# A mixed SSM and MLP kernel: u stored in quarters, Bu's fourth product and the output block's second product put earlier

## Chip, cores and metric

The kernel runs on one core of a Trainium2 chip. The metric is device time in microseconds, from the first to the last instruction and what lies around them; lower is better. Engines are named as in the profile: PE does matmuls, PEld loads their weights, DVE is the vector engine, ACT the scalar engine, POOL is GpSimd, and SP issues loads.

## The reference

The input x has 2048 rows of 1024. One path is a diagonal complex state-space model: an input product Bu, a recurrence along the 2048 rows, and an output product with C. The other is a layer norm and an MLP of width 3584 with gelu. A gate for each row mixes them.

```python
Bu = jnp.einsum("bld,pd->blp", x + 0j, B_bar)
...
for t in range(L):
    h = Lam_bar[None, :] * h + Bu[:, t, :]
...
y = 2.0 * jnp.einsum("blp,dp->bld", hseq, Cmat).real + x * Dskip[None, None, :]
...
y = _layernorm(x, axis=-1)
h = _gelu(jnp.einsum("bsd,df->bsf", y, w1) + b1)
return jnp.einsum("bsf,fd->bsd", h, w2) + b2
...
return g * a + (1 - g) * b
```

## The kernel before

Every large product is cut in a two by two grid and done with seven products instead of eight, in the way of Strassen and Winograd. A group (class SG) has the seven as p1 to p7, in three PSUM banks: p1 and p2 share bank a, p5 and p3 share bank e, and p6, p7 and p4 share bank b. ACT copies p1's bank into bank b ahead of p6 (the seed, L904). ACT also copies bank e after p5 (s5) and bank b after p6 (su) to SBUF (L888, or L889 with a factor). The function fin of each kind of group takes the four results out: after p2, p3, p7 and p4. A later product on a bank waits until the earlier result in it has been read. Sums of inputs that S and T operands need are made by DVE (dve_tt, L932).

Four kinds of groups follow each other on PE. Bu groups (bu_group, 4 matmuls a product) make u for 8 tiles of 128 states, in two halves of the rows, after four plain products (bu_plain). Then come blocks of m groups (MLP up, 4 matmuls a product, gelu on ACT at L1318 and L1324, DVE's addition at L1322), b groups (MLP down, 7 matmuls, results at L1402 and L1405, stored to scr_ac as partial sums at L1412 and, accumulating, L1414), and at the end the 8 y groups (output product, 8 matmuls, results at L1501 and L1503). Products of neighbouring groups are interleaved: a group's p7 and p4 stand among the next group's products.

u goes from ACT and DVE (L1010, L1016, L1019 with L1021) to a ring of two slots in SBUF, and from there to scratch in HBM by stores on POOL's queue (u_store, L947). The scan (ssm, on DVE: L1198, L1201, L1212) loads u for four tiles and 256 rows at a time (L1185) and stores its result on POOL's queue (L1230). POOL also makes the layer norm's statistics (L1051 to L1056) and stores the normalised rows (L1063), which DVE makes at L1061.

The order on each engine isn't written by hand but for PE's. Each operation is a task with an engine, a guessed duration and a priority; PE's products are chained in the order in which the code makes them. Graph.schedule plays the tasks through with the guessed durations and fixes the order of every engine's list, SP's and POOL's queues among them. On the chip each engine works through its list in order and waits on semaphores. POOL_ISSUE is the guessed duration of a DMA issue on POOL. So a change of a guess or of PE's order can change the lists of all engines.

Buffers lie in one arena and overlap: the fourth of the sums for y groups with an even number (ysq, index 3) ends 1 KB inside the first slot of the ring from which the b groups' partial sums are stored. The planner makes the later writer wait for the earlier reader.

Of the kernel before, what the change touches and what calls it, by code (L numbers as in the profile page):

```python
# [25 lines left out]
ACT_ISSUE = 0.12  # L26
POOL_ISSUE = 1.2
XPOSE_ISSUE_PER_MB = 3.8
# [391 lines left out]
def build(nc, A_x, A_Lambda_re, A_Lambda_im, A_B_re, A_B_im, A_C_re, A_C_im, A_log_dt, A_Dskip,  # L420
          B_x, B_w1, B_b1, B_w2, B_b2, gate_w, out, stats=None):
# [5 lines left out]
    CH = 512  # L427
    NCH = L // CH
    DT = D // 128
    PT = P // 128  # L430
# [4 lines left out]
    T = 256  # L435
# [8 lines left out]
    g = Graph()  # L444
    es = ExitStack()
    with es:
# [9 lines left out]
        US = nc.dram_tensor("scr_u", (PT // 4, 128, L // T, 8 * T), BF16, kind="Internal").ap()  # L456
# [36 lines left out]
        EV0 = AO + 10240  # L493
# [440 lines left out]

        b_us = [[[B("us%d_%d_%d" % (p, c, r)) for r in range(2)] for c in range(NCH // 2)] for p in range(PT)]
        b_hs = [[B("hs%d_%d" % (p, h)) for h in range(L // T)] for p in range(PT // 4)]
# [6 lines left out]

        def u_store(pt, pr, ks, q, ri):
            evv = AR.v(EV0 + ks * 4096 + ri * 2048, [(T, 4), (1, T)])
            r0 = ((pt % 4) * 2 + ri) * T
            g.dma((1.0, q), lambda e: e.dma_start(out=US[pt // 4, :, 4 * pr:4 * pr + 4, r0:r0 + T], in_=evv.ap), 2 * 128 * CH * 2,  # L947
                  ssem("us", 2 * ks + ri, True), reads=[evv], writes=[b_us[pt][pr][ri]], name="us%d.%d.%d" % (pt, pr, ri), q="pool")

        cev = {}  # L950

        def bu_plain(pt, c):

            if c % 2 == 0:
                cev[pt, c // 2] = nxt("ev", NEV)
            ks = cev[pt, c // 2]
            for ri in range(2):
                bk = (4, 5, 6, 0, 1, 2)[nxt("cbank", 6)]
                ws = [AR.v(bqo(pt, 2 * ri) + dt * 256, [(1, 128)]) for dt in range(DT)]
                q = mm("bu%d.%d.%d" % (pt, c, ri), bk, ws, [xt(dt, c) for dt in range(DT)], True)  # L960
                ev = u_ev(pt, c // 2, ks, ri, c % 2)
                g.add("act", c_act(CH), (1.0, q), lambda e, ev=ev, bk=bk: e.activation(ev.ap, V(PS[bk], 0, [(1, 2 * T)]), AF.Copy),  # L962
                      reads=[b_ps[bk]], writes=[ev, b_ps[bk]], name="u%d.%d.%d" % (pt, c, ri))
                if c % 2 == 1:
                    u_store(pt, c // 2, ks, q, ri)

# [19 lines left out]
        def bu_group(pt, pr):  # L986
# [15 lines left out]
            bu_n[0] += 1  # L1002
            done = {}

            def fin(qd, q, bk):
# [6 lines left out]
                else:  # L1012
# [5 lines left out]
                    else:  # L1018
# [3 lines left out]
                              reads=[uc, sv], writes=[ev], name="u" + nm)  # L1022
                done[qd] = True
                if done.get(2 * ri) and done.get(2 * ri + 1):
                    u_store(pt, pr, ks, q, ri)
            return SG("_u%d.%d" % (pt, pr), st, mv, fin, su, s5)
# [99 lines left out]
        for n, (pt, pr) in enumerate(order):  # L1126
# [14 lines left out]
            cur.p5()  # L1141
            cur.p6()
            cur.p2()
            cur.p3()
            if prev is not None:
                prev.p4()
                opt = order[n - 1][0]
                if order[n - 1][1] == 1 and opt < 3:
                    bT_dma(opt + 5)
# [26 lines left out]
        def ssm(pg, q):  # L1176
# [5 lines left out]
            def pri(i):  # L1182
                return (50.0, un, i)
            uf = AR.v(so, [(1, UE)])
            g.dma((50.0, un), lambda e: e.dma_start(out=uf.ap, in_=US[pg, :, q, :]), UE * 128 * 2,  # L1185
                  ssem("sb", s), reads=[b_us[4 * pg + a][q // 4] for a in range(4)], writes=[uf], name="ul" + tag)

# [369 lines left out]
        for n, it in enumerate(flat):  # L1557
# [19 lines left out]
            if kind == "y":  # L1577
                if x + 1 < 8:
                    y_prep(x + 1, seq[0] + 4)
            early2 = kind == "b" and x == 0  # L1580
            if early2:
# [28 lines left out]
            if last_of_block:  # L1610
                if nit is None:
                    prev.p4()
                else:
                    nk = blocks[nit[0]][0]
                    if nk == "b":
# [9 lines left out]
                        pend = make((nit[0], nit[1] + 1))  # L1625
                        pend.p1()
                    else:
                        cur = make(nit)
# [59 lines left out]
```

## Time and profile before

| | |
|---|---|
| median of 3 runs | 558.57 us (558.56 to 558.93) |
| the profiled execution's own time | 558.57 us |
| its span | 556.8 us |
| PE busy | 548.0 us (98%) |
| DVE busy | 511.8 us (92%) |
| ACT busy | 283.1 us (51%) |
| POOL busy | 92.1 us (17%) |
| granted TensorE clock | 1.000 |

The span is the time from the first to the last instruction that the profile has; the execution's own time is 1.8 us longer. Busy time is summed over an engine's instructions. A row of a timeline gives start, duration, engine, line, operation and count; in brackets stands the idle time of the engine before it and what ended it. Consecutive instructions of DVE and ACT overlap by some 0.08 to 0.13 us. Matmuls overlap too, so a row's duration reaches a little into the next.

### The profile page before, as it was taken

The page shows a single profiled execution, that of the slowest core. Times are in us where ns is not written, and L with a number is a line of the kernel's source. Part 1 is how long each engine was busy: PE and PEld are TensorE (multiplying, and loading weights), DVE is VectorE, ACT ScalarE, POOL GpSimd, SP SyncE. Part 2 cuts the span into 40 slices and gives each one's busy share as a digit, 9 for nine tenths or more (in the row PEclk, how much of TensorE's full clock was granted, in tenths as well). Part 3 has the DMA queues.
Part 4 walks back from the last instruction along what each step waited for, and adds up shares of the span by engine and source line. Part 5 has one row for each costly group of instructions (what it writes and reads, how often), then busy time and mean ns, then how long its engine had stood idle before and what let it go on. Part 6 is the DMA issues. An engine that isn't in the chain of part 4 may idle for free.

```text
span 556.8 us, 7435 instructions
## 1 busy us (share of the span) xinstructions
PE 548.0 (98%) x2610; PEld 248.5 (45%) x2610; DVE 511.8 (92%) x867; ACT 283.1 (51%) x477; POOL 92.1 (17%) x146
## 2 busy tenths in 40 slices
PE   8999999989999999999999999999999999999997
PEld 5544444434444444444444444444444444444443
DVE  4999999999999999999999999999999867988873
ACT  3968899647774347674246753246662322111110
POOL 0226636630001110011110000220000211001000
DMA  9998999799492345576546866787669999686521
GB/s 263 243 310 204 260 283 275 235 354 328 151 226 97 135 185 181 169 233 230 208 163 197 284 142 156 140 196 196 201 159 257 233 286 320 215 325 238 191 99 57
DMA packets 114911, 120.08 MB, mean 216 GB/s; under 512 B 70322, under 2 KB 92594, under 8 KB 113850
## 3 DMA queue, kind: packets, MB, share of 16 engines
q1 hardware_dynamic: 102256, 73.69, 48.0%
q0 software_dynamic: 12480, 45.90, 26.5%
q8 instruction: 20, 0.33, 0.2%
q14 instruction: 17, 0.14, 0.1%
q10 hardware_dynamic: 138, 0.02, 0.0%
HBM read 56.40 MB, written 47.46 MB: 187 GB/s over the span
## 4 chain that ended last, share of the span: by engine, by line
PE 80%; DVE 13%; issue 2%; DMA 2%; POOL 2%; ACT 0%; DVEq 0%; ACTq 0%; POOLq 0%
PE ps L871 59%; PE ps L869 19%; DVE ar L932 3%; DMA scr_ac<-ar 2%; DVE ar L1212 2%; DVE ar L1198 2%; DVE ar L1061 1%; DVE ar L1016 1%; DVE ar L1021 1%; PE ps L686 1%; DVE ar L1201 1%; POOL cst L1052 1%; DVE ar L1322 1%; POOL scr_u L947 1%; DVE ar L852 1%
## 5 line engine op out<-in xcount | busy, mean ns | idle before, releaser
L871 PE MATMUL ps<-ar 128*128 128x512 f16 (+1 forms) x1832 | 414.3, 379 | 4.3 <-ACT ps L904 2.4
L871 PEld LDWEIGHTS ps<-ar 128*128 128x128 f16 (+1 forms) x1832 | 178.2, 98 | 223.2 <-ACT ps L904 4.2
L869 PE MATMUL ps<-ar 128*128 128x512 bf16 (+1 forms) x640 | 156.9, 379 | 0.1
L932 DVE TENSOR_TENSOR ar<-ar 128x512 f16<-128x512 bf16 (+6 forms) x216 | 138.9, 684 | 6.4 <-DMA scr_ac<-ar 4.9
L869 PEld LDWEIGHTS ps<-ar 128*128 128x128 bf16 (+1 forms) x640 | 62.2, 98 | 74.9 <-issue 0.4
L1212 DVE TENSOR_TENSOR_SCAN ar<-cst,init,ar 128x256 bf16<-128x256 f32 x128 | 88.8, 735 | 0.5
L888 ACT ACTIVATE ar<-ps 128x512 f32<-128x512 f32 x100 | 58.6, 594 | 50.2 <-PE ps L869 36.8
L1198 DVE TENSOR_TENSOR ar<-ar 128x2048 bf16<-128x2048 bf16 x64 | 77.0, 1218 | 0.1
L904 ACT ACTIVATE ps<-ps 128x512 f32<-128x512 f32 x66 | 38.5, 584 | 66.5 <-PE ps L869 61.9
L1318 ACT ACTIVATE ar<-ps,cst 128x512 bf16<-128x512 f32 x56 | 38.4, 687 | 21.5 <-PE ps L871 20.9
L889 ACT ACTIVATE ar<-ps,cst 128x512 f32<-128x512 f32 x32 | 22.0, 688 | 45.0 <-PE ps L871 19.3
L1324 ACT ACTIVATE ar<-ar,cst 128x512 bf16<-128x512 f32 x56 | 40.0, 714 | 7.7 <-DVE ar L1322 7.5
L1201 DVE TENSOR_TENSOR ar<-ar 128x1024 bf16<-128x1024 bf16 x64 | 42.7, 685 | 0.3
L1402 ACT ACTIVATE ar<-ps,cst 128x512 f32<-128x512 f32 x32 | 22.0, 687 | 41.2 <-PE ps L871 41.2
L1322 DVE TENSOR_TENSOR ar<-ps,ar 128x512 f32<-128x512 f32 x56 | 38.2, 682 | 3.3 <-PE ps L871 3.0
L947 POOL DMA_DIRECT2D scr_u<-ar x32 | 24.7, 774 | 62.1 <-ACT ar L962 22.8
L1503 DVE SCALAR_TENSOR_TENSOR ar<-ps,cst,ar 128x512 bf16<-128x512 f32 x32 | 23.8, 748 | 11.7 <-PE ps L871 11.6
L1230 POOL DMA_DIRECT2D scr_h<-ar x16 | 9.0, 564 | 125.4 <-DVE ar L1201 125.2
L1414 POOL DMA_DIRECT2D scr_ac<-ar x16 | 13.8, 892 | 81.2 <-DVE ar L1405 37.9
L1405 DVE SCALAR_TENSOR_TENSOR ar<-ps,cst,ar 128x512 f32<-128x512 f32 x32 | 23.8, 742 | 3.5 <-PE ps L871 3.2
L1482 DVE SCALAR_TENSOR_TENSOR ar<-ar,cst 128x1024 f32<-128x1024 bf16 x16 | 20.3, 1279 | 0.0
L1412 POOL DMA_DIRECT2D scr_ac<-ar x16 | 8.5, 532 | 69.2 <-DVE ar L1405 28.0
(110 smaller groups left out, 241.9 us busy)
## 6 DMA issues: line engine op xcount, KB each, us to landing
scr_ac<-ar POOLq DMA_DIRECT2D x32, 512.0 KB, 5.2
ar<-in_A_x_dram SPq DMA_DIRECT2D x32, 256.0 KB, 5.6
scr_u<-ar POOLq DMA_DIRECT2D x32, 256.0 KB, 5.3
ar<-scr_u SPq DMA_DIRECT2D x16, 512.0 KB, 5.2
scr_h<-ar POOLq DMA_DIRECT2D x16, 512.0 KB, 5.8
ar<-scr_ac SPq DMA_DIRECT2D x16, 512.0 KB, 6.9
ar<-scr_h SPq DMA_DIRECT2D x8, 1024.0 KB, 6.7
ar<-in_B_w_dram SPq DMA_DIRECT2D x14, 512.0 KB, 6.5
```

The source lines that it names most:

```text
L869: ins = e.matmul(V(PS[bk], 0, [(1, n)]), st[i].ap, mv[i].ap, start=(i == 0), stop=(i == K - 1))
L871: ins = e.matmul(V(PS[bk], 0, [(1, n)]), st[i].ap, mv[i].ap, start=False, stop=(i == K - 1), skip_group_check=True)
L888: return e.activation(o.ap, V(PS[bk], 0, [(1, 512)]), AF.Copy)
L904: g.add("act", c_act(512), (pb[0], q - 2), lambda e: e.activation(V(PS[b], 0, [(1, 512)]), V(PS[a], 0, [(1, 512)]), AF.Copy), reads=[b_ps[ ...
L932: g.add("dve", c_tt16(n), (pb[0], q), lambda e: e.tensor_tensor(o.ap, a.ap, b.ap, op), reads=[a, b], writes=[o], name=nm).slack = slack
L947: g.dma((1.0, q), lambda e: e.dma_start(out=US[pt // 4, :, 4 * pr:4 * pr + 4, r0:r0 + T], in_=evv.ap), 2 * 128 * CH * 2, ssem("us", 2 * ks ...
L1198: g.add("dve", c_tt16(UE), pri(i), lambda e: e.tensor_tensor(o.ap, a.ap, tbl.ap, ALU.mult), reads=[a, tbl], writes=[o], name=nm + tag)
L1201: g.add("dve", c_tt16(UE // 2), pri(i), lambda e: e.tensor_tensor(o.ap, a.ap, b.ap, op), reads=[a, b], writes=[o], name=nm + tag)
L1212: lambda e, pt=pt, ri=ri, vin=vin, go=go: e.tensor_tensor_scan(go.ap, Cb("R", pt, T), vin.ap, V(INIT, pt * 2 + ri, [(1, 1)]), ALU.mult, AL ...
L1318: g.add("act", c_act(512, ap_operands=1), (10.0, q + 1), lambda e: e.activation(o.ap, V(PS[bk], 0, [(1, 512)]), AF.Gelu_apprx_tanh, bias=C ...
L1322: g.add("dve", c_dve(512), (10.0, q - 2), lambda e: e.tensor_tensor(sv.ap, V(PS[bk], 0, [(1, 512)]), sv.ap, ALU.add), reads=[b_ps[bk], sv] ...
L1324: g.add("act", c_act(512, psum=False, ap_operands=1), (10.0, q + 3), lambda e: e.activation(o.ap, sv.ap, AF.Gelu_apprx_tanh, bias=C("B1", ...
```

## The change

Five edits. A store of u now carries 512 rows of one part (real or imaginary) of a tile and not 1024, and is issued as soon as these are there; 32 stores of 256 KB become 64 of 128 KB, with a semaphore each for the eight places of the ring, and a scan load waits only for the stores that hold its rows. POOL_ISSUE goes from 1.2 to 0.8. In the Bu loop the fourth product of the group before stands ahead of the second and third of the current one, and not behind them. At the start of the y block the first y group's second product stands ahead of its fifth, and the last b group's fourth stands ahead of both, where the fifth stood.

```diff
-POOL_ISSUE = 1.2
+POOL_ISSUE = 0.8
...
-        def u_store(pt, pr, ks, q, ri):
-            evv = AR.v(EV0 + ks * 4096 + ri * 2048, [(T, 4), (1, T)])
+        def u_store(pt, c, ks, q, ri):
+            evv = AR.v(EV0 + ks * 4096 + (ri * 4 + 2 * (c % 2)) * T * 2, [(T, 2), (1, T)])
             r0 = ((pt % 4) * 2 + ri) * T
-            g.dma((1.0, q), lambda e: e.dma_start(out=US[pt // 4, :, 4 * pr:4 * pr + 4, r0:r0 + T], in_=evv.ap), 2 * 128 * CH * 2,
-                  ssem("us", 2 * ks + ri, True), reads=[evv], writes=[b_us[pt][pr][ri]], name="us%d.%d.%d" % (pt, pr, ri), q="pool")
+            g.dma((1.0, q), lambda e: e.dma_start(out=US[pt // 4, :, 2 * c:2 * c + 2, r0:r0 + T], in_=evv.ap), 128 * CH * 2,
+                  ssem("us", 4 * ks + 2 * ri + c % 2, True), reads=[evv], writes=[b_us[pt][c][ri]], name="us%d.%d.%d" % (pt, c, ri), q="pool")
...
-                if c % 2 == 1:
-                    u_store(pt, c // 2, ks, q, ri)
+                u_store(pt, c, ks, q, ri)
...
-                done[qd] = True
-                if done.get(2 * ri) and done.get(2 * ri + 1):
-                    u_store(pt, pr, ks, q, ri)
+                u_store(pt, 2 * pr + c, ks, q, ri)
...
             cur.p5()
             cur.p6()
+            if prev is not None:
+                prev.p4()
             cur.p2()
             cur.p3()
             if prev is not None:
-                prev.p4()
                 opt = order[n - 1][0]
...
-                  ssem("sb", s), reads=[b_us[4 * pg + a][q // 4] for a in range(4)], writes=[uf], name="ul" + tag)
+                  ssem("sb", s), reads=[b_us[4 * pg + a][q // 2] for a in range(4)], writes=[uf], name="ul" + tag)
...
-            early2 = kind == "b" and x == 0
+            early2 = kind != "m" and x == 0
...
+                    elif nk == "y":
+                        cur = make(nit)
+                        prev.p7()
+                        cur.p1()
+                        prev.p4()
                     else:
                         cur = make(nit)
                         prev.p7()
                         cur.p1()
                         cur.p5()
                         early5 = True
                         prev.p4()
```

The lists that the planner makes of this differ in many places up to about a third of the program. Line numbers of the changed kernel are 2 to 4 lower from L1010 on and up to L1565.

PE's list where the last b group hands over to the first y group, before. ps4 is b's bank b; ps1, ps2 and ps5 are y's banks a, e and b. The rows are y's first, y's fifth, b's fourth, y's sixth and y's second product.

```order
L869 MATMUL ps1<-ar 128x512 x8
L869 MATMUL ps2<-ar 128x512 x8
L871 MATMUL ps4<-ar 128x512 x7
L871 MATMUL ps5<-ar 128x512 x8
L871 MATMUL ps1<-ar 128x512 x8
```

The same place in the changed kernel.

```order
L869 MATMUL ps1<-ar 128x512 x8
L871 MATMUL ps4<-ar 128x512 x7
L871 MATMUL ps1<-ar 128x512 x8
L869 MATMUL ps2<-ar 128x512 x8
L871 MATMUL ps5<-ar 128x512 x8
```

b's fourth product has moved ahead of y's fifth, and y's second ahead of y's fifth and sixth.

ACT's list at the start of the first m block, before. The rows are the gelu of the first group's second product, the last u, the gelu of its third product (L1324, on what DVE has added), the second group's seed (ps0 to ps4), its copies s5 and su, and the gelu of the first group's seventh product.

```order
L1318 ACTIVATE ar<-ps1,cst 128x512
L1010 ACTIVATE ar<-ps5 128x512
L1324 ACTIVATE ar<-ar,cst 128x512
L904 ACTIVATE ps4<-ps0 128x512
L888 ACTIVATE ar<-ps3 128x512
L888 ACTIVATE ar<-ps4 128x512
L1324 ACTIVATE ar<-ar,cst 128x512
```

The same place in the changed kernel (L1315, L1008 and L1321 are L1318, L1010 and L1324 of before).

```order
L1315 ACTIVATE ar<-ps1,cst 128x512
L1008 ACTIVATE ar<-ps5 128x512
L904 ACTIVATE ps4<-ps0 128x512
L1321 ACTIVATE ar<-ar,cst 128x512
L888 ACTIVATE ar<-ps3 128x512
L1321 ACTIVATE ar<-ar,cst 128x512
L888 ACTIVATE ar<-ps4 128x512
```

The seed has moved ahead of the gelu, and the second gelu ahead of the copy su.

DVE's list at the same place, before, from the last u addition (L1021) on. L1201 and L1198 belong to the scan, L932 with 128x512 are the sums of a w1 tile, and L1322 are the additions ahead of gelus.

```order
L1021 TENSOR_TENSOR ar<-ar 128x512
L1201 TENSOR_TENSOR ar<-ar 128x4x256
L1322 TENSOR_TENSOR ar<-ps,ar 128x512
L1225 TENSOR_TENSOR init<-init,fxt 128x8
L1201 TENSOR_TENSOR ar<-ar 128x4x256
L1198 TENSOR_TENSOR ar<-ar 128x2048
L932 TENSOR_TENSOR ar<-ar 128x512 x3
L1322 TENSOR_TENSOR ar<-ps,ar 128x512
```

The same place in the changed kernel (L1019, L1319, L1218, L1220 and L1195 are L1021, L1322, L1221, L1223 and L1198 of before).

```order
L1019 TENSOR_TENSOR ar<-ar 128x512
L1218 TENSOR_TENSOR fxt<-ar,cst 128x8
L1195 TENSOR_TENSOR ar<-ar 128x2048
L1220 TENSOR_TENSOR init<-ar,cst 128x8
L1195 TENSOR_TENSOR ar<-ar 128x2048
L932 TENSOR_TENSOR ar<-ar 128x512 x3
L1319 TENSOR_TENSOR ar<-ps,ar 128x512
```

The u addition has moved ahead of two scan products, the three w1 sums have moved ahead of the first addition L1322, and one scan combination (L1201) behind it.

## Rows read from the trace of the kernel before

**Rows 1.** The page: span, and busy time, share and instructions of each engine.

```profile
span 556.8 us, 7435 instructions
PE 548.0 (98%) x2610; PEld 248.5 (45%) x2610; DVE 511.8 (92%) x867; ACT 283.1 (51%) x477; POOL 92.1 (17%) x146
```

**Rows 2.** Busy time of the engines in a stretch; stretch and length come first.

```profile
core 0: us, PE busy (x) PEld busy (x) DVE busy (x) ACT busy (x) POOL busy (x), PEclk, DMA share, GB/s
19.00:130.00 111.00, 107.91 (x523) 47.45 (x521) 109.63 (x235) 85.79 (x161) 54.39 (x79) 1.00 1.02 275
```

**Rows 3.** Waits of PE: total us, times, longest us.

```profile
PE ps L871 <- ACT ps L904: 2.4, 2, 2.1
PE ps L871 <- DVE ar L1405: 0.7, 1, 0.7
```

**Rows 4.** Timeline around 123 us, PE, then ACT, then DVE.

```profile
123.71 3.63 PE L871 MATMUL ps<-ar 128*128 128x512 f16 x16 [2.14 <-ACT ps L904]
...
122.45 0.72 ACT L1324 ACTIVATE ar<-ar,cst 128x512 bf16<-128x512 f32 x1 [2.84 <-DVE ar L1322]
123.08 0.58 ACT L904 ACTIVATE ps<-ps 128x512 f32<-128x512 f32 x1
123.59 0.58 ACT L888 ACTIVATE ar<-ps 128x512 f32<-128x512 f32 x1
...
120.53 0.69 DVE L1021 TENSOR_TENSOR ar<-ar 128x512 bf16<-128x512 f32 x1
121.13 0.68 DVE L1201 TENSOR_TENSOR ar<-ar 128x1024 bf16<-128x1024 bf16 x1
121.73 0.69 DVE L1322 TENSOR_TENSOR ar<-ps,ar 128x512 f32<-128x512 f32 x1
124.14 1.09 DVE L932 TENSOR_TENSOR ar<-ar 128x512 f16<-128x512 bf16 x3
```

**Rows 5.** Timeline from 454 to 460 us, PE, then DVE.

```profile
454.60 1.89 PE L869 MATMUL ps<-ar 128*128 128x512 bf16 x8
456.33 1.89 PE L869 MATMUL ps<-ar 128*128 128x512 f16 x8
458.92 2.33 PE L871 MATMUL ps<-ar 128*128 128x512 f16 x10 [0.71 <-DVE ar L1405]
...
457.51 0.69 DVE L932 TENSOR_TENSOR ar<-ar 128x1024 f16<-128x1024 bf16 x1 [4.89 <-DMA scr_ac<-ar]
458.12 0.74 DVE L1405 SCALAR_TENSOR_TENSOR ar<-ps,cst,ar 128x512 f32<-128x512 f32 x1
```

**Rows 6.** The chain of work that ended last: start, duration, what.

```profile
444.30 13.19 DMA scr_ac<-ar
```

**Rows 7.** Timeline around 35 us, DVE, then PE.

```profile
35.71 2.35 DVE L932 TENSOR_TENSOR ar<-ar 128x2048 f16<-128x2048 bf16 x2
...
34.88 3.40 PE L871 MATMUL ps<-ar 128*128 128x512 f16 x15
```

**Rows 8.** Timeline around 140 and 163 us, DVE, then PE.

```profile
139.11 0.69 DVE L1322 TENSOR_TENSOR ar<-ps,ar 128x512 f32<-128x512 f32 x1
162.34 1.15 DVE L932 TENSOR_TENSOR ar<-ar 128x896 f16<-128x896 bf16 x2
...
141.85 1.46 PE L871 MATMUL ps<-ar 128*128 128x512 f16 x6
163.69 1.67 PE L871 MATMUL ps<-ar 128*128 128x512 f16 x7
```

**Rows 9.** Timeline of DVE, its two longest waits between 50 and 130 us.

```profile
56.98 1.46 DVE L1061 TENSOR_SCALAR ar<-ar,cst 128x1024 bf16<-128x1024 bf16 x3 [0.47 <-POOL cst L1056]
...
128.88 0.69 DVE L1604 TENSOR_TENSOR ar<-ar 128x512 f32<-128x512 bf16 x1 [0.38 <-DMA ar<-in_B_b_dram]
```

**Rows 10.** Timeline of SP's queue at 114 us, then line L1273's issues to landing.

```profile
114.71 0.37 SPq L1273 DMA_DIRECT2D ar<-in_B_w_dram  x1
...
DMA to landing us min/median/max: 3.7/6.5/8.6
```

**Rows 11.** Lines L1061, L947 and L1063: shortest, median and longest ns, first and last start.

```profile
L1061 DVE TENSOR_SCALAR ar<-ar,cst x16: 527/551/842, 57.0 to 105.2; 128x1024 bf16<-128x1024 bf16 x16
L947 POOL DMA_DIRECT2D scr_u<-ar x32: 750/757/924, 23.7 to 121.7; - x32
L1063 POOL DMA_DIRECT2D scr_xn<-ar x16: 540/552/727, 57.8 to 112.5; - x16
```

More of the change, by code (lines that the diff above doesn't have):

```diff
@@ L932, in dve_tt @@
             g.add("dve", c_tt16(n), (pb[0], q), lambda e: e.tensor_tensor(o.ap, a.ap, b.ap, op), reads=[a, b], writes=[o], name=nm).slack = slack
-        b_us = [[[B("us%d_%d_%d" % (p, c, r)) for r in range(2)] for c in range(NCH // 2)] for p in range(PT)]
+        b_us = [[[B("us%d_%d_%d" % (p, c, r)) for r in range(2)] for c in range(NCH)] for p in range(PT)]
         b_hs = [[B("hs%d_%d" % (p, h)) for h in range(L // T)] for p in range(PT // 4)]
@@ L1002, in bu_group @@
             bu_n[0] += 1
-            done = {}
             def fin(qd, q, bk):
```

## The prediction, made before the run

> **What bounds the kernel now.** I read the page first. PE is busy for 548.0 of 556.8 us, and DVE for 511.8 [rows 1]: whatever the change does, it can save only time in which PE waits, and it can lose wherever a product is put before its input. The share of DVE is an average, so I read it by stretches next. From 19 to 130 us DVE is busy for 109.63 of 111.00 us [rows 2]: there DVE runs down its own list without a pause, and a product that needs one of its results gets it at a time that PE cannot influence. PE's own waits came third [rows 3]: for ACT's seed copies (L904) two waits, 2.4 us, and for DVE's L1405 one, 0.7 us. The timeline shows where these two stand, and the edits that the new order brings meet them both.
>
> The first is near 123.7 us, in the second group of the first m block (m1). PE idles for 2.14 us before m1's sixth product [rows 4]. That product needs the seed copy at 123.08 on ACT, and the copy stands behind a gelu at 122.45, which waits for the DVE addition that starts at 121.73 (L1322). So this wait ends when DVE reaches that addition.
>
> The second is where the last b group hands over to y. Product seven of b ends at 454.60, y's first product takes 454.60 to 456.33, y's fifth 456.33 to 458.06 (8 matmuls each, so 1.73 us for eight and 0.216 for one), and b's fourth product starts at 458.92 [rows 5]. What it waits for is DVE's addition at 458.12 (L1405), which empties the bank that it writes. That addition is itself late, because DVE works in order and stood for 4.89 us before the y sum at 457.51 (L932). The chain names the cause: a store of partial sums, issued at 444.30, that takes 13.19 us to land, until 457.49 [rows 6]; the y sum's tile overlaps the tile that this store reads.
>
> **The change part by part, the y order.** Before, y's first and fifth products stood between b's seventh and b's fourth; now only the first does, with y's second and fifth behind b's fourth. The DVE order there is the same up to that addition, and so are the POOL and SP orders, so the store is issued, lands, and frees DVE at the same distance from PE's work as now. b's fourth product therefore starts at 458.92 as now, but with 1.73 us less work done ahead of it: the wait grows from 0.86 (458.92 less 458.06) to 2.59 (458.92 less 456.33). Behind it stand two y products and not one before y's sixth. Nothing later gives it back, because PE has no further wait from there to its end. Cost: +1.73. Its bounds are nothing, if the store lands 2.6 us sooner, and 1.73.
>
> **The Bu order and the planner's new list.** The fourth product of each Bu group moves ahead by two products of four matmuls, 1.73 us. It accumulates into the bank that ACT or DVE must have read after its seventh product, and it needs the fourth sum of x. In one group that sum is too late: DVE makes it from 35.71, 1.22 us of a pair that takes 2.35 with 0.08 of overlap, thus to 36.93; the row of PE that starts with the sixth product at 34.88 lets the fourth start at 34.88 + 0.86 = 35.74 [rows 7]. A new wait of 1.2 us. It does not reach the end. PE idles for 3.09 of the 111 us to 130 [rows 2], 2.14 of them at m1 and the rest on the way there, and these waits end when ACT and DVE reach something, not when PE does; a PE that comes 1.2 later waits that much less at them.
>
> At m1 the new ACT order puts the seed copy ahead of the gelu. The sixth product no longer waits for the addition of DVE; but ACT's copy of the fifth product (L888) still stands behind the gelu, and m1's third product needs that. So the wait moves two products of 0.86 further. When does DVE reach the addition? In its new list the three sums of the next w1 tile (1.09 us together, 1.01 net of overlap) stand ahead of it, and one combination of 0.68 (0.60 net, the step to the next row) has gone behind it: 0.41 later, ending at 122.82 instead of 122.41 [rows 4]. From that end to a product behind gelu and copy PE took 123.71 - 122.41 = 1.30. The third product then starts at 124.12, against 123.71 + 1.73 = 125.44 now: 1.32 won at this place.
>
> Not all of it lasts. With PE ahead and DVE as now, the next additions of DVE come just in time. Two places are the tightest. In the fourth group (m3) the sixth product starts at 141.85 now, and the addition before it ends at 139.11 + 0.69 = 139.80; with 1.25 for gelu and copy PE can gain at most 0.8. At the first b group the fifth product starts at 163.69 and the sum that it reads is ready at 162.96 (first of two in the row at 162.34, 1.15 long with 0.08 of overlap): at most 0.7 [rows 8]. Past 173 us DVE waits for PE many times and follows it, so 0.7 is kept to the end, if DVE's list up to there takes as long as now.
>
> Whether it does is the unknown. It now holds two waits, 0.47 for POOL's statistics and 0.38 for the b2 load [rows 9]; if both vanish DVE is 0.85 earlier and the gain is 1.5. On the other side, the new list reaches loads earlier. The w1 sums, at 124.14 now, come at about 121.1 (122.82 less 0.61 and 1.01); their load is issued at 114.71 and such loads take 3.7, 6.5 or 8.6 us (least, middle, most) [rows 10], so it is there at 118.4 to 123.3, and its issue waits for stores of xn that stand behind more POOL issues than now. That is a DVE wait of 0 to 2.2; I take 0.5. The b2 load is issued when DVE's last u addition has ended (L1021, at 120.53 now); in the new list both that addition and the reader come about 2.4 earlier, so its 0.4 stays. For the transposes of B's later tiles, which are read earlier as well, I add 0.2 by choice. Together 1.1 against 0.85: DVE is about 0.2 later, and the gain is 0.7 - 0.2 = 0.5. Its ends are 1.5 and, with the full 2.2 at the w1 load, a loss of 1.2.
>
> **The stores and their price.** 32 stores of 256 KB, 0.75 us of POOL each (median 757 ns) become 64 of half the size. A store of xn, the same bytes in a quarter of the pieces, takes POOL 0.55, so a half is put between 0.55 and 0.76 [rows 11]; at 0.65 POOL's work grows by 64 x 0.65 - 32 x 0.76 = 17 us. POOL is busy for 54 of the 111 us to 130 [rows 2], so this fits, and nobody on PE waits for POOL. The first scan loads come earlier, and DVE has other work then anyway, so I give this nothing. The planner's number for an issue changes only the order, which is counted above.
>
> Sum, against the profiled run's own 558.57 (a span of 556.8 and 1.8 around it; it equals the median of the three runs): 558.57 + 1.73 - 0.5 = 559.8.
>
> **The rivals.** (a) DVE keeps its 0.85: the three loads are there in time. The gain is 1.5, the time 558.57 + 1.73 - 1.5 = 558.8. For it speaks that the loads' transfers find fewer others under way. (b) DVE falls behind by 1 to 2 us through one of those loads; then PE's 0.7 becomes a loss of 0.3 to 1.3: 560.6 to 561.6. (c) POOL's issues hold DVE up. The xn normalisations (L1061) take 527 ns at least and 842 at most, and POOL issues xn and u stores in the same stretch [rows 11]. If 8 of the 16 go from shortest to longest, DVE loses 8 x 0.315 = 2.5 more, and PE's gain of 0.5 becomes a loss of 2.0: 558.57 + 1.73 + 2.0 = 562.3. The Trainium skill's page SBUF — State Buffer, section "Who interferes with whom", says that a DVE instruction in a two-port mode and GpSimd exclude each other for a whole instruction, and that tensor_tensor takes only the read side of the shared pair; by it twice the issues would cost DVE time at its one-input operations. The spread of L1061 agrees with that; what the two-input operations do beside an issue no row here tells. (d) On the other side: the store of partial sums lands early. If it lands 2.6 us sooner than 457.49, before y's first product ends, b's fourth product waits for nothing, and the 0.86 of now goes too: 558.57 - 0.86 - 0.5 = 557.2. It is decided at a landing of 10.6 us after the issue and less. Against it: the transfers around it are the same and in the same order. (e) The wait at 35.7 isn't absorbed: 559.8 + 1.2 = 561.0.
>
> **How the numbers follow.** A difference under 0.2%, 1.1 us, is about what a measurement of this kernel cannot tell from none. Chances: the forecast (559.2 to 560.4) 0.42, (a) 0.25, (b) 0.14, (c) 0.04, (d) 0.08, (e) 0.07. Slower by more than 1.1 us, above 559.7, are (b), (c), (e) and somewhat over half of the forecast's range: 0.49. Faster, under 557.5, is (d): 0.08. The rest, 0.43, is no difference. The range leaves out (d) and the far part of (b) and (c): 558.4 to 561.2.
>
> **What the changed profile would show.** If the y step is right, PE's longest wait is for DVE's L1405 before b's fourth product, 2.4 to 2.7 us, with DVE standing before a y sum until a scr_ac store lands. If the m step is right, there is no wait before m1's sixth product and one of 1 to 2 us before its third, for ACT's L888. DVE's waits between 50 and 130 us, summed, say whether (a) or (b) holds: under 0.4, or over 2. The store at (d) shows in its time to landing. The forecast is wrong if b's fourth product starts without a wait, or if m1's third starts later, against the work done, than now.

## The result, and the profile after

The changed kernel takes 565.64 us (median of 4 runs, 565.03 to 567.57), the kernel before 558.57; the ratio is 1.0132, with a 95% interval of 1.0107 to 1.0157. It is 7.1 us slower, where 1.2 were forecast with a range up to 561.2. All ratios here leave out the few executions in a slower state, and they are not the quotient of the medians beside them. The page of its profiled run (565.8) answers to [rows 1]:

```profile
span 564.1 us, 7422 instructions
PE 547.4 (97%) x2562; PEld 249.5 (44%) x2610; DVE 510.2 (90%) x867; ACT 284.1 (50%) x477; POOL 114.1 (20%) x178
```

The work of PE and DVE is that of before (48 matmul records are missing, so a matmul's row can be one short); only POOL does 22 us more. So the 7.3 us of span are waiting, or work at a slower clock. PE's waits, against [rows 3]:

```profile
PE ps L871 <- DVE ar L1402: 3.4, 1, 3.4
PE ps L871 <- ACT ar L888: 2.0, 1, 2.0
PE ps L871 <- ACT ps L904: 1.6, 1, 1.6
PE ps L871 <- DVE ar L932: 1.1, 1, 1.1
```

L1402 is the former L1405 (lines behind the edits stand two to four lower). The timeline says where they are, PE's rows of the m block first, then ACT's and DVE's there, then PE's and DVE's at y:

```profile
120.53 1.89 PE L871 MATMUL ps<-ar 128*128 128x512 f16 x7
124.41 2.43 PE L871 MATMUL ps<-ar 128*128 128x512 bf16 x8 [1.99 <-ACT ar L888]
129.56 1.03 PE L869 MATMUL ps<-ar 128*128 128x512 f16 x4
132.23 2.12 PE L871 MATMUL ps<-ar 128*128 128x512 f16 x9 [1.64 <-ACT ps L904]
...
130.97 0.72 ACT L1321 ACTIVATE ar<-ar,cst 128x512 bf16<-128x512 f32 x1 [3.41 <-DVE ar L1319]
131.59 0.58 ACT L904 ACTIVATE ps<-ps 128x512 f32<-128x512 f32 x1
...
129.64 0.69 DVE L1601 TENSOR_TENSOR ar<-ar 128x512 f32<-128x512 bf16 x1 [3.18 <-DMA ar<-in_B_b_dram]
130.25 0.68 DVE L1319 TENSOR_TENSOR ar<-ps,ar 128x512 f32<-128x512 f32 x1
...
462.73 5.10 PE L871 MATMUL ps<-ar 128*128 128x512 f16 x15 [3.40 <-DVE ar L1402]
467.66 1.89 PE L869 MATMUL ps<-ar 128*128 128x512 f16 x8
...
461.32 0.69 DVE L932 TENSOR_TENSOR ar<-ar 128x1024 f16<-128x1024 bf16 x1 [5.86 <-DMA scr_ac<-ar]
```

Read upwards from PE's wait before 132.23 (m4's sixth product; before, it started at 129.76): the seed copy of ACT at 131.59 stands behind a gelu that waits for DVE's addition at 130.25 (L1319), and that addition (of m1's third product, m1's own first) stands behind the difference of the two b2 halves (L1601), for which DVE waits 3.18 us. In [rows 9] the same instruction waited 0.38, at 128.88, and the addition of m1's third product was ahead of it:

```profile
127.22 0.69 DVE L1322 TENSOR_TENSOR ar<-ps,ar 128x512 f32<-128x512 f32 x1
```

A word on names: the expectations below call this addition "m1's second addition", or "m1's addition" where they speak of b2. Their "m1's first addition", and "m1's addition" where they speak of the w1 sums, is an earlier one that m1's products wait for, the addition of m0's third product (121.73 in [rows 4]).

The chain names the two transfers that end last, with their time under way:

```profile
119.50 10.11 DMA ar<-in_B_b_dram
447.65 13.65 DMA scr_ac<-ar
```

The windows show the third part, in the column PEclk (the granted clock, 1.00 is 2.4 GHz and 0.50 is 1.2 GHz):

```profile
core 0: us, PE busy (x) PEld busy (x) DVE busy (x) ACT busy (x) POOL busy (x), PEclk, DMA share, GB/s
125.40:129.10 3.70, 3.70 (x11) 1.31 (x9) 1.06 (x1) 1.75 (x4) 0.57 (x1) 0.54 0.88 207
463.50:467.00 3.50, 3.50 (x10) 1.22 (x8) 0.97 (x2) 0.69 (x1) 0.71 (x1) 0.51 1.06 257
467.00:470.00 3.00, 3.00 (x15) 1.37 (x14) 1.69 (x3) 0.33 (x1) 0.14 (x1) 1.00 1.01 378
...
100.00:110.00 10.00, 10.00 (x48) 4.56 (x47) 8.13 (x17) 5.84 (x10) 9.01 (x13) 1.00 0.37 124
110.00:119.00 9.00, 8.95 (x42) 4.07 (x42) 9.00 (x14) 4.95 (x9) 7.16 (x12) 1.00 0.95 329
119.00:126.00 7.00, 4.95 (x22) 2.13 (x22) 7.00 (x15) 3.10 (x6) 1.82 (x3) 0.97 0.97 363
```

In the kernel before, the clock is 1.00 in all of these stretches. Here PE waits, starts again, and 1 us later works at half speed for 3.5 us or so. The Trainium skill, TensorE: Matmul & The Clock Gate, section "HAM oscillation — how this bites in real kernels", tells the same sequence for a kernel that waits for its loads: a wait, and the products behind it at the lower clock. The two stretches agree, but for the first 0.8 to 1.0 us behind each wait, which still have the clock at 1.00.

Now the account can be made, from the starts of the same product in both traces. The rows of the kernel before are m0's seventh product, m4's sixth and the first of the second y group; those of the changed kernel, behind the dots, are the first and the last of these:

```profile
119.68 1.03 PE L871 MATMUL ps<-ar 128*128 128x512 f16 x4
129.76 3.62 PE L871 MATMUL ps<-ar 128*128 128x512 f16 x16
465.62 1.89 PE L869 MATMUL ps<-ar 128*128 128x512 bf16 x8
...
118.80 1.03 PE L871 MATMUL ps<-ar 128*128 128x512 f16 x4
472.84 1.89 PE L869 MATMUL ps<-ar 128*128 128x512 bf16 x7
```

At m0's seventh product PE is 0.88 ahead (118.80 against 119.68). At m4's sixth it is 2.47 behind (132.23 against 129.76). Small waits up to y add 0.37: b's seventh product starts at 455.93 against 453.09 (worked out from y's first product at 0.216 a matmul), 2.84 behind. Behind b's fourth product and y's first group it is 7.22 behind (472.84 against 465.62), and so it stays. So 2.8 us are lost by the end of the b blocks, nearly all in the m block, and 4.4 at y.

### The profile page after: what moved, and what is told of

It is laid out like the page before. It is cut to its first block, busy times and chain, and to the rows that moved or that the text cites. A ratio compares the mean times of both kernels' runs of the same rounds, so it can differ in the third digit from the quotient of the medians.

```text
span 564.1 us, 7422 instructions
## 1 busy us (share of the span) xinstructions
PE 547.4 (97%) x2562; PEld 249.5 (44%) x2610; DVE 510.2 (90%) x867; ACT 284.1 (50%) x477; POOL 114.1 (20%) x178
## 4 chain that ended last, share of the span: by engine, by line
PE 75%; DVE 16%; DMA 4%; issue 3%; ACT 2%; POOL 0%; SPq 0%; DVEq 0%; ACTq 0%; POOLq 0%
PE ps L871 57%; PE ps L869 17%; DVE ar L932 7%; DMA scr_ac<-ar 2%; DVE ar L1319 2%; DVE ar L1209 2%; DMA ar<-in_B_b_dram 2%; DVE ar L1195 1%; DVE ar L809 1%; ACT ar L674 1%; PE ps L686 1%; DVE ar L1198 1%; DVE ar L658 0%; ACT ar L962 0%; PE ps L654 0%
## 5 line engine op out<-in xcount | busy, mean ns | idle before, releaser
L871 PE MATMUL ps<-ar 128*128 128x512 f16 (+1 forms) x1799 | 415.2, 381 | 10.7 <-DVE ar L1402 3.4
L932 DVE TENSOR_TENSOR ar<-ar 128x512 f16<-128x512 bf16 (+6 forms) x216 | 138.6, 682 | 7.5 <-DMA scr_ac<-ar 5.9
L1195 DVE TENSOR_TENSOR ar<-ar 128x2048 bf16<-128x2048 bf16 x64 | 77.0, 1217 | 0.0
L947 POOL DMA_DIRECT2D scr_u<-ar x64 | 46.9, 733 | 42.4 <-ACT cst L747 10.6
L1315 ACT ACTIVATE ar<-ps,cst 128x512 bf16<-128x512 f32 x56 | 38.4, 686 | 23.7 <-PE ps L871 23.2
L1321 ACT ACTIVATE ar<-ar,cst 128x512 bf16<-128x512 f32 x56 | 40.0, 715 | 11.2 <-DVE ar L1319 10.8
L1198 DVE TENSOR_TENSOR ar<-ar 128x1024 bf16<-128x1024 bf16 x64 | 42.5, 684 | 0.3
L1319 DVE TENSOR_TENSOR ar<-ps,ar 128x512 f32<-128x512 f32 x56 | 38.1, 681 | 3.4 <-PE ps L871 2.9
L1402 DVE SCALAR_TENSOR_TENSOR ar<-ps,cst,ar 128x512 f32<-128x512 f32 x32 | 23.7, 741 | 3.9 <-PE ps L871 3.8
```

Of the source, the lines that this page charges most:

```text
L871: ins = e.matmul(V(PS[bk], 0, [(1, n)]), st[i].ap, mv[i].ap, start=False, stop=(i == K - 1), skip_group_check=True)
L932: g.add("dve", c_tt16(n), (pb[0], q), lambda e: e.tensor_tensor(o.ap, a.ap, b.ap, op), reads=[a, b], writes=[o], name=nm).slack = slack
L947: g.dma((1.0, q), lambda e: e.dma_start(out=US[pt // 4, :, 2 * c:2 * c + 2, r0:r0 + T], in_=evv.ap), 128 * CH * 2, ssem("us", 4 * ks + 2 * ...
L1195: g.add("dve", c_tt16(UE), pri(i), lambda e: e.tensor_tensor(o.ap, a.ap, tbl.ap, ALU.mult), reads=[a, tbl], writes=[o], name=nm + tag)
L1198: g.add("dve", c_tt16(UE // 2), pri(i), lambda e: e.tensor_tensor(o.ap, a.ap, b.ap, op), reads=[a, b], writes=[o], name=nm + tag)
L1315: g.add("act", c_act(512, ap_operands=1), (10.0, q + 1), lambda e: e.activation(o.ap, V(PS[bk], 0, [(1, 512)]), AF.Gelu_apprx_tanh, bias=C ...
```

## The experiments

"Before" and "changed" are the two kernels. Where a kernel differs from one of them by the place of an instruction in an engine's list, a method that takes an entry out of the list and puts it behind another does it (`move(engine, entry, behind)`, called after the scheduler). The times, each beside the runs of the kernel before on the same chip:

| Kernel | us, median | before | ratio, 95% interval |
|---|---|---|---|
| a_yold: changed, y order of before | 562.48 | 559.56 | 1.0066 [1.0041, 1.0090] |
| a_b2d: changed, b2 difference moved back | 563.27 | 559.56 | 1.0072 [1.0048, 1.0097] |
| b_y: before, y order alone | 562.07 | 559.56 | 1.0055 [1.0029, 1.0080] |
| a_ac: changed, y's fourth sum moved | 565.33 | 559.56 | 1.0085 [1.0048, 1.0122] |
| b_ac: before, y's fourth sum moved | 558.56 | 559.42 | 0.9993 [0.9957, 1.0028] |
| a_fix: changed, all places mended | 558.51 | 559.42 | 0.9980 [0.9959, 1.0002] |
| b_bu: before, Bu order alone | 559.27 | 559.42 | 0.9998 [0.9972, 1.0024] |
| b_st8: before, stores by quarters and 0.8 | 574.25 | 559.42 | 1.0256 [1.0219, 1.0293] |
| b_iss: before, 0.8 alone | 569.73 | 558.87 | 1.0201 [1.0177, 1.0225] |
| b_st: before, stores by quarters alone | 581.05 | 558.87 | 1.0397 [1.0379, 1.0415] |
| b_bu2: b_bu, one more execution | 558.87 | 558.87 | one run |
| b_best: before, Bu order, two moves | 555.89 | 558.47 | 0.9945 [0.9931, 0.9959] |

**a_yold.** The changed kernel without the last two pieces of the diff.

```
-            early2 = kind != "m" and x == 0
+            early2 = kind == "b" and x == 0
...
-                    elif nk == "y":
-                        cur = make(nit)
-                        prev.p7()
-                        cur.p1()
-                        prev.p4()
```

> The changed kernel with the order of products at y as it was before. Theory: of the 7.1 us lost, 4.4 are lost at the hand-over from b to y (order 1.7, a store that lands 1.0 later against the work done, half the granted clock for 3.5 us behind the wait 1.7) and 2.8 in the m block, where the b2 load lands 10.1 us after its issue. Undoing the y order alone then gives 565.6 - 4.4 = 561.2 to 562.2 (the later store may still cost its 1.0), with the granted clock at 1.00 around 464 us. Rival: the wait at y comes from the stores and not from the order of products; then the wait before b's fourth product stays above 2.5 us, the clock falls again and the time stays above 563.

```profile
PE ps L871 <- DVE ar L1402: 1.4, 1, 1.4
```

The wait before b's fourth product falls from 3.4 to 1.4, the clock is 1.00 from 459 to 467, and PE loses 0.7 at y instead of 4.4. By the ratios, 1.0132 to 1.0066, the y order costs 3.7 us here. The theory holds, though 1.0066 of 558.57 is 562.3, a little above its 561.2 to 562.2. The wait is 0.7 above that of [rows 3]: the store, issued at 447.57, takes 13.41 us and not 13.19, and is issued 0.5 later against y's first product (457.37).

**b_y.** The same two pieces, with the opposite signs, on the kernel before.

> The kernel before with the y order alone. Theory A (the sum on record): b's fourth product waits 2.6 us and nothing else changes, +1.73, 560.3. Theory B: the clock falls to half behind a wait of this length, as in the changed kernel, and costs 1.7 more: 562.0. Theory C: the order itself costs nothing and the loss at y belongs to the stores by quarters: under 559.2.

PE's timeline, and the window behind the wait:

```profile
454.19 1.89 PE L869 MATMUL ps<-ar 128*128 128x512 bf16 x8
458.55 5.10 PE L871 MATMUL ps<-ar 128*128 128x512 f16 x15 [2.47 <-DVE ar L1405]
463.48 0.81 PE L869 MATMUL ps<-ar 128*128 128x512 f16 x3
```

```profile
459.40:463.00 3.60, 3.60 (x11) 1.40 (x10) 0.90 (x2) 0.69 (x1) 0.86 (x1) 0.56 1.05 268
```

Theory B. The wait is 2.47 against 0.71, 1.76 more, which is the forecast term; and 15 matmuls then take 463.48 - 458.55 = 4.93 us. At full clock the same fifteen take 3.23 (next run). So the half clock costs 1.70, as much as the order. Together 3.46, in the profiled run; 0.55%, or 3.1 us, over the runs, between 1.6 and 4.5 by the interval, so it is the profile that tells B from A.

**a_ac.** One DVE entry of the changed kernel moved: `move("dve", "ys4_0", "ac1.3.3")`, y's fourth sum behind L1402's addition.

> The changed kernel with one DVE instruction moved: y's fourth sum, whose tile lies on a slot that a store of partial sums still reads, goes behind the addition that empties the bank of b's fourth product. Theory: the wait of 3.4 us before b's fourth product and the half clock behind it both go, the new y order costs nothing by itself, and the time is 565.6 - 3.6 - 1.7 = 560.4 (560.0 to 561.0). Rival: the y products behind wait for the same store instead, since they need the y sums that now stand behind it on DVE; then the wait moves by a product or two and less than 2 us is won, 563.5 or more.

```profile
464.59 3.40 PE L871 MATMUL ps<-ar 128*128 128x512 f16 x15
467.82 1.89 PE L869 MATMUL ps<-ar 128*128 128x512 f16 x8
...
128.14 1.10 DVE L932 TENSOR_TENSOR ar<-ar 128x512 f16<-128x512 bf16 x3 [6.42 <-DMA ar<-in_B_w_dram]
```

At y the theory holds: no wait before b's fourth product, no half clock, and PE gains 0.88 there on the kernel before although the new y order is in. The time is another matter. The runs go from 560.86 to 567.89, and the profiled one (567.02) shows why it can be so: the w1 load, issued at 111.72, took 16.40 us, and the three w1 sums, which in the changed list stand ahead of the addition of m0's third product, held DVE up for 6.42. In the profile of the changed kernel the same load took 5.7. That the other long runs have the same cause is not shown.

**a_b2d.** `move("dve", "b2d", "vr0.2")` on the changed kernel: the b2 difference behind the addition of m1's third product and the scan's next pair.

> The changed kernel with one DVE instruction moved: the difference of the two b2 halves goes behind the addition of m1 and the next combination pair of the scan, as in the kernel before. Theory: the 2.5 us lost between m1 and m4 are DVE standing for the b2 load with m1's addition behind it; PE's wait of 1.6 before m4's sixth product goes, and the time falls by 1.6 if the granted clock is still 0.5 for 3 us behind m1's third product (then that half clock is the next thing that binds, 564.0), by 2.5 to 3.3 if it is not (562.3 to 563.1). Rival: DVE just stands for the load one place later and what is behind it comes as late as now: no gain, 565.0 or more.

```profile
124.59 1.90 PE L871 MATMUL ps<-ar 128*128 128x512 bf16 x8 [2.01 <-ACT ar L888]
128.91 3.62 PE L871 MATMUL ps<-ar 128*128 128x512 f16 x16
139.57 1.04 PE L869 MATMUL ps<-ar 128*128 128x512 bf16 x4 [0.61 <-DMA ar<-in_B_w_dram]
```

```profile
124.60:130.00 5.40, 5.40 (x26) 2.45 (x27) 4.97 (x8) 4.17 (x7) 0.57 (x1) 1.00 0.89 247
```

m4's sixth product starts at 128.91, not 132.23, with no wait: PE is 0.85 ahead of the kernel before and not 2.47 behind. The time, 1.0072 of 558.57 or 562.6, is in the second range of the theory. It gives 1.2 back by 140, 0.6 of it to a w1 load that the fourth scan load has got ahead of on SP (in a_fix, where that load goes behind, this wait is not there). The clock stayed at 1.00 here behind a wait of the same 2.0 us, so this run does not tell what the half clock in the m block would have cost without its cover; in the changed kernel it cost nothing, since PE waited for the b2 load behind it in any case.

**b_bu and b_bu2.** The third piece of the diff alone (the fourth product ahead).

> The kernel before with the Bu order alone. Its DVE list has the b2 difference ahead of m1's second addition, but the w1 sums and the seed copy stay where they were. Theory: the wait of 1.2 us at 36.8 us is taken back before 124 us, m1's sixth product waits as before, and DVE stands for the b2 load near 127 us with the addition behind it, so m4's sixth product waits 1 to 1.7 us: 1 to 1.7 us slower than the kernel before. Rival: the load is there in time without the stores by quarters, and the time is that of the kernel before within 0.5 us.

> A second look at the kernel before with the Bu order alone, whose first profile fell on an execution 4.5 us above its median. Theory: in an execution near the median (558.9 to 559.5) PE waits 1.2 us at 36.8 us, has made that good before 124 us, and waits under 1 us at m4. Rival: it waits as long at m1 and m4 as in the first profile, 3.7 and 1.0 us, and wins the time elsewhere.

The profile of the first fell on its longest execution (563.78, against a median of 559.27), in which the w1 load held DVE up for 3.6 us. The second profile, near the median:

```profile
121.71 3.63 PE L871 MATMUL ps<-ar 128*128 128x512 f16 x15 [1.07 <-ACT ps L904]
129.58 2.76 PE L871 MATMUL ps<-ar 128*128 128x512 f16 x12 [1.66 <-ACT ps L904]
...
126.99 0.69 DVE L1605 TENSOR_TENSOR ar<-ar 128x512 f32<-128x512 bf16 x1 [2.23 <-DMA ar<-in_B_b_dram]
```

PE waits 1.08 at 36.72, is ahead again by 113 us, and m1's sixth product starts 2.0 us earlier than in [rows 4]. Then DVE stands 2.23 for the b2 load with the addition of m1's third product behind it, and 1.8 of the 2.0 are gone at m4. I had expected under 1 us there: the wait is 1.7. Over its twelve runs b_bu takes the time of the kernel before (0.9998, by the interval 1.3 us more at most), where 1 to 1.7 us more were expected. The rival had the time right and the reason wrong, since the load is late; what the theory missed is the 2.0 us won up to m1. In this profile the place of one DVE instruction takes nearly all of it back; b_best, below, moves that instruction.

**b_iss, b_st, b_st8.** The planner's number alone, the stores alone, and both. For b_iss:

```
-POOL_ISSUE = 1.2
+POOL_ISSUE = 0.8
```

> The kernel before with the planner's number for a POOL issue alone (0.8 for 1.2). Its list puts the three w1 sums ahead of m1's addition, and of five more DVE instructions than in the changed kernel; the b2 difference stays far behind. By the kernel before, DVE gets there at 118.1 us and the w1 load lands at 121.9. Theory: DVE stands 3 to 4 us for that load, m1's addition comes about 4.5 later and m1's third product with it, less the 1.7 of products that have gone ahead: 2.5 to 4 us slower than the kernel before. Rival: the load's issue moves ahead too, nobody stands, and the time is within 0.7 us of the kernel before.

> The kernel before with the stores by quarters alone, the planner's number at 1.2. The planner then believes POOL to be late by 38 us and puts m1's first addition behind 12.3 us more of DVE work. Theory: the planner's list and not the transfers makes the time, so PE waits about 12 us at m1 less what DVE has already done of later work, 8 to 14 us slower than the kernel before. Rival: PE waits less than 5 us there, because the scan's pieces that went ahead are what DVE must do anyway.

> The changed kernel with the Bu order and the y order of before, so the stores by quarters and the planner's smaller number alone. Its DVE list has the w1 sums two places ahead of m1's first addition and the b2 difference ahead of the second. Theory: the loss in the m block belongs to this part's new list, so DVE stands for one of the two loads for 1 to 4 us and PE's lag at m4 is 1.5 to 4 us; the y part stays at its 0.9 to 1.6 us wait. Rival: the stores cost nothing and the list matters little, and the time is within 1 us of the kernel before.

DVE's waits from 50 to 140 us in b_iss, then PE's in b_st, then in b_st8:

```profile
DVE ar L932 <- DMA ar<-in_B_w_dram: 4.9, 1, 4.9
DVE ar L1061 <- POOL cst L1056: 3.9, 1, 3.9
```

```profile
PE ps L869 <- DVE ar L932: 18.0, 3, 13.2
PE ps L871 <- DVE ar L932: 4.5, 2, 4.2
```

```profile
PE ps L869 <- DMA ar<-scr_h: 10.7, 1, 10.7
```

In b_iss DVE waits for the w1 load, 4.9 and not 3 to 4, and earlier 3.9 for POOL's statistics, which I had not seen coming; 10.9 us slower, not 2.5 to 4. In b_st PE waits 13.2 before m0, not m1, for sums that the list put behind other work, and 22.5 in all. The place was another and the size was underestimated; that the list and not a transfer makes the time held, as DVE waits for no DMA from 50 to 140 us. In b_st8 the loss at m4 is 2.4 us, as in the changed kernel, with DVE standing 2.2 for b2; the rest is one store of a scan (L1226) that POOL's list has behind four stores of partial sums, so that a load at y comes 10.7 late. In all three the longest waits traced here go back to the place of an instruction in a list: the w1 sums, m0's sums, a scan's store. What the new stores cost apart from the lists no run tells.

**b_ac.** The move of a_ac on the kernel before.

> The kernel before with one DVE instruction moved: y's fourth sum goes behind the addition that empties the bank of b's fourth product. Theory (the wait of 0.87 us there is nothing but that sum standing for the store): the wait goes, 0.9 us faster than the kernel before. Rival: the addition waits for another store too (its bank's sum goes into a tile that a store still reads), and the wait stays at 0.5 or more: no change.

The wait before b's fourth product is gone in the profile, and PE gains 0.88 there (0.07 behind the profiled run of before at b's seventh product, 0.81 ahead at y's). The interval of the runs, 0.9957 to 1.0028, is too wide to say so.

**a_fix.** `move("dve", "b2d", "vr0.2")`, the w1 sums behind the addition of m0's third product, `move("dve", "ys4_0", "ac1.3.3")`, and on SP `move("sp", "ul0.3", "w1_3")`.

> The changed kernel with the engine orders mended at the places where its time was lost: on DVE the b2 difference behind the scan's next pair and the three w1 sums behind m1's addition (as in the kernel before), y's fourth sum behind the addition of b's fourth product; on SP the fourth scan load behind the load of the next w1 tile, which it delays. Theory: all of the 7.1 us are in these places; PE's lag against the kernel before is -0.7 at the first b block and -1.5 behind y, and the time is 1 to 1.6 us under the kernel before. Rival: the stores by quarters fill the DMA engines between 100 and 140 us, and a wait for another transfer takes the place of these; then it stays 1 us or more above the kernel before.

558.51: the 7 us are gone, and its runs lie within 557.84 to 559.60. So the loss is in these places together, but the gain over the kernel before is not clear of noise (0.998, up to 1.0002). PE still waits 1.0 and 0.4 at m1 and 0.4 at m2, and its distances were not those expected: 0.3 behind the kernel before at the first b block and not 0.7 ahead, and 0.5 ahead behind y and not 1.5.

**b_best.** What the runs point to: the Bu order on the kernel before, without the new stores, number and y order, and the two moves of DVE entries.

```
             cur.p6()
+            if prev is not None:
+                prev.p4()
             cur.p2()
             cur.p3()
             if prev is not None:
-                prev.p4()
...
+        g.move("dve", "b2d", "vr0.2"); g.move("dve", "ys4_0", "ac1.3.3")
```

> The kernel before with the Bu order and two DVE instructions moved: the b2 difference behind the scan's next pair, and y's fourth sum behind the addition of b's fourth product. Theory: in the look at the Bu order alone m1 came 2.0 us ahead of the kernel before and DVE's standing for the b2 load took 1.8 of it back; with that instruction behind m1's second addition PE stays ahead by what the next additions of DVE allow, 0.7 at the first b block, and the 0.9 at y goes too: 1.3 to 1.7 us under the kernel before. Rival: DVE, which runs without pauses there, gives the time back elsewhere before the first b block, and only y's 0.9 is won.

```profile
463.16 1.89 PE L869 MATMUL ps<-ar 128*128 128x512 bf16 x7
```

555.89 us, 0.9945 of the kernel before (0.9931 to 0.9959), the fastest of all; that is 2.3 to 3.9 us, where 1.3 to 1.7 were expected. PE is 1.65 ahead at the first b block and 2.46 ahead behind y (463.16 against 465.62). I had allowed 0.7 at the b block. DVE has no wait over 0.2 us between 50 and 140 us here, where it had 0.85 before; rival (a) put a gain of 1.5 on that, and 1.65 is near it, though this kernel has neither the new stores nor the new number. No run has the Bu order and the b2 move without the move at y.

## Why the prediction was wrong, step by step

The sum had +1.73 at y and -0.5 in the m block. PE lost 4.4 at y and 2.8 by the end of the b blocks.

**The Bu order** was right: the new wait is 1.05 us in the timeline at 36.79 (1.2 forecast), and PE has made it good by 100 us.

**The m step** was right as far as m1: no wait before the sixth product, and the third starts at 124.41, forecast 124.12. Two slips on the way change no term by more than 0.1: 122.82 less 0.61 and 1.01 is 121.2 and not 121.1, and m3 is the fifth group of its block (m0, m1, m4, m2, m3), not the fourth.

**"Both that addition and the reader come about 2.4 earlier, so its 0.4 stays"** is the step that failed, and it holds two errors. The first: an earlier issue was taken for an earlier landing. The load was issued 2.2 us earlier (119.50 against 121.68), took 10.1 us instead of 7.2, and landed 0.8 later, 129.62 against 128.86. The windows show the DMA engines full from 110 us on, at shares of 0.95 and 0.97; the kernel before has 1.01 and 0.93 there. From 100 to 110 us, though, the share is 0.37 where it was 0.78:

```profile
100.00:110.00 10.00, 10.00 (x48) 4.58 (x47) 9.90 (x18) 6.25 (x11) 7.26 (x10) 1.00 0.78 256
```

There the changed order of POOL leaves a hole: a scan's store (issued at 114.67, not 103.11), a w1 store (112.13, not 103.71) and the load of the fourth scan piece (123.02, not 106.17) now fall into the full stretch. The Trainium skill, DMA: Bandwidth & Descriptors, section "Issuing engines are not separate DMA queues", says that transfers of all issuers interleave on the same 16 engines; by that a POOL store that comes later can delay an SP load. But most of the longer landing comes without the hole. b_bu2 has the old stores, the scan's store at 101.56 and the scan load at 104.86, and from 100 to 110 us its DMA share is 0.71; yet its b2 load, issued 3.8 us earlier than in the kernel before, took 9.12 us:

```profile
100.00:110.00 10.00, 10.00 (x48) 4.58 (x47) 9.87 (x19) 5.89 (x10) 6.54 (x10) 1.00 0.71 231
...
117.85 9.12 DMA ar<-in_B_b_dram
```

So 1.9 of the 2.9 us by which the load grew slower come without the hole. Of the three transfers only the w1 store is late in b_bu2 too (110.89); no run moves it alone, and why the load takes longer stays open. The second error: the reader was priced as a wait of DVE. The new DVE list, behind the stretch of it that is shown with the change, has this reader ahead of the addition of m1's third product, so the wait went to ACT and PE behind it. a_b2d shows it: the one instruction moved back, and the 3.3 us at m4 are won.

**The y term, +1.73,** had the right mechanism and is one part of three. b_y has its 1.76. "At the same distance from PE's work as now" failed by 1.0 us in the changed kernel: against y's first product, the store is issued 0.5 later and takes 0.5 longer (13.65 against 13.19). The third part, the half clock behind the wait, 1.70, was in no term and no rival. The sum of the three is 1.73 + 0.97 + 1.70 = 4.4, what PE lost at y.

**The stores' price** was low, and the cover partly wrong. The rows of a half and of the normalisations after:

```profile
L947 POOL DMA_DIRECT2D scr_u<-ar x64: 706/723/888, 12.0 to 120.1; - x64
L1057 DVE TENSOR_SCALAR ar<-ar,cst x16: 534/540/555, 56.7 to 105.3; 128x1024 bf16<-128x1024 bf16 x16
```

A half takes 723 ns and not 650, so half the bytes cost POOL nearly the price of the whole, 757 [rows 11]; POOL's work grows by 22 us, forecast 17. PE waits for POOL only for 1.4 us at the start, as in the kernel before, but DVE does later: its waits from 50 to 130 us are

```profile
DVE ar L1601 <- DMA ar<-in_B_b_dram: 3.2, 1, 3.2
DVE ar L1057 <- POOL cst L1052: 2.5, 2, 1.8
```

2.5 us for POOL's statistics, 0.47 before. With the 3.2 this is well over the 2 us that were to mean rival (b); (b) was the right kind of rival, but its loss of 0.3 to 1.3 for PE came out as 2.5. The wait for the statistics has no part in that: a_b2d has the same 2.5, and PE is 0.85 ahead there at m4. Of the others, (e) fell, since the wait at 36.8 was made good; (d) fell, since the store landed later and not sooner; and **rival (c)** did not come: with twice the stores of u on POOL, the normalisations on DVE took 555 ns at most against 842. Eight of the sixteen lie wholly beside issues of stores on POOL and take 535 to 555, while one beside none takes 547 ns, so the cost put on them there is not seen. What made the longest ones long before is not shown.

## What to carry to other kernels

On an engine that works through a list in order, price a load by what stands behind its reader, not by the reader's own wait, and check each reader that the new order has moved ahead. Where the DMA engines are full, as here at shares of 0.9 and more, do not take an earlier issue for a landing as much earlier: give such a load its spread (5.7 to 16.4 us for one w1 load here) before an engine is made to depend on it. At y, waits of PE of 2.5, 3.3 and 3.4 us (b_y, a_b2d, the changed kernel) each cost 1.7 us more at the half clock behind them, whatever their length; a reorder that adds such a wait has to price that too, unless another wait behind it covers the loss, as in the m block.

## What the runs showed that was not expected

How long a wait must be for the clock to fall did not come out as one number. Behind waits of 0.7 and 1.4 us at y it stayed at 1.00, and behind 2.5, 3.3 and 3.4 it fell to 0.50. In between it went both ways: with 2.0 at m1 it fell in the changed kernel and in a_yold and stayed in a_b2d, and with 2.1 it stayed in the kernel before. What else decides it is left open.

The same load, issued within 0.3 us of the same place with the same neighbours, landed after 5.7 us in the profile of the changed kernel and after 16.4 in that of a_ac. Why is left open too. An order that depends on such a load may be a matter of luck: a_ac's runs spread over 7 us where a_fix's, in which the w1 sums stand one addition later, spread over 1.8; that the load makes this spread is not shown.
